# Causal decay attention into a gated feed-forward net: the order of work where the one hands over to the other, the order of two weight loads, and x in six arrays instead of one

## The chip, the cores and the metric

The kernel runs on one core of a Trainium2 chip. The metric is the device time of one execution in microseconds; the median of three executions stands for a kernel. A profiled execution gives a trace of every instruction; its span (first to last record) is a little shorter than its device time.

## The reference

Inputs are q, k and v of 8 batches x 8 heads x 576 tokens x 64, a forget factor f per token, and two weights. Cut to what matters:

```python
scores = q @ k.T / 8
cum = cumsum(log(clip(f, 1e-4, 1)))
scores = where(causal, -1e9, scores + cum[:, None] - cum[None, :])
attn = softmax(scores)
x = (attn @ v), heads side by side             # 4608 tokens x 512
h = x @ w_in                                   # 512 x 2048
g = h * erf(softplus(h))
y = g @ w_out                                  # 2048 x 512
```

## The kernel before

**Attention.** A pair is two heads of one batch; there are 32 pairs, p = 0 to 31, and each is done in two halves, t = 2p and 2p + 1, so t runs from 0 to 63 (`NH` is 64). Half t goes through stages in successive turns of one loop: scores on TensorE and their reduction on VectorE (turn t), exponentials on ScalarE (t + 1), `normalize` on GpSimd (t + 2), `transposes` on TensorE into PSUM banks of a ring of three and `evacuate` out of them (t + 3), `values` on TensorE (t + 4), and `store`, VectorE copies out of PSUM (t + 4 or t + 5). The transposes of an even half fill three banks (12 matmuls), those of an odd half four (13). `values` has one PSUM bank, so the next `values` waits for the copies of `store`. The odd half's store issues one DMA that writes 128 rows x 576 tokens of x to the DRAM array `xt_d` (512 x 4608). `evacuate` uses ScalarE for banks 0 and 1 and VectorE for 2 and 3. Turns 64 to 67 (the loop runs to `NH + 4`) drain the last halves.

**Feed-forward.** Tokens are taken 768 at a time (a visit k), features 256 at a time; one such piece is a unit u, 48 in all. A unit is `up(u, 0)` and `up(u, 1)` (42 matmuls into four PSUM banks a, b, x, y; seven products of a Strassen-like scheme with each operand split into a high and a low part), `activate` (ScalarE: four softplus, four erf, with a table load ahead of each kind), `gate` (VectorE: erf times h), `round_gate` (ScalarE rounds to the high part `gh`, GpSimd subtracts for the low part `gl`), and `down` (36 matmuls with `wo`, the weights of w_out, into `y`). One PSUM bank per name a, b, x, y exists, so `up(u + 1)` waits for the last reader of the bank of unit u; that of bank a is gate 0. `load_wi` and `load_wo` fetch a unit's weights from DRAM into two SBUF buffers each. `load_x` fetches a visit's x in four quarters from `xt_d`; `sub`, `high` and `low` make operands of it on GpSimd and ScalarE.

**The handover.** Turns 64 and 65 put `up(0, 0)` and `up(0, 1)` among the last attention halves; turn 65 ends with `activate(0)` and the gates of unit 0; turn 66 transposes half 63, does `values(62)`, then `up(1, 0)`; turn 67 does `up(1, 1)`, then `values(63)` and its store. After the loop come the pools of the feed-forward stage (`wop` is the first of them, where attention's pool `wk` lay, whose first tiles are the probabilities `pr`), `load_wo(0)`, `load_wo(1)`, `load_wi(3)`, and then, for each unit, `middle` (down, activate and gates of the next unit), and `up(u + 2)`.

**What sets the order.** TensorE, VectorE, ScalarE and GpSimd run in the order in which the Python code issues their instructions. SP, which issues all DMAs but one, is not in that list (`ORDERED`): the framework's planner puts its DMAs in order by when it thinks they can start, and SP then takes them strictly one after another, waiting for each. Each DMA uses one of eight semaphores in turn, so it also waits for the DMA eight before it.

Of the kernel before, what the change touches and what calls it, by code (L numbers as in the profile page):

```python
# [11 lines left out]
F32 = mybir.dt.float32  # L12
# [9 lines left out]
P = 128  # L22
B, H, S, D = 8, 8, 576, 64
NT = B * S
DM = H * D
# [27 lines left out]
TB = 384  # L53
NW = 2 * TB
NV = NT // NW
# [18 lines left out]
class Moe:  # L74
# [38 lines left out]
    def load_x(self, k):  # L113
        if k >= len(self.visits):
            return
        for nm in ("11", "12", "22", "21"):
            i, j = int(nm[0]) - 1, int(nm[1]) - 1
            self.raw[k, nm] = r = self.half(nm, k)
            c = self.visits[k][0] * NW + j * TB
            self.nc.sync.dma_start(out=r, in_=self.xt_d[2 * i * P:2 * (i + 1) * P, c:c + TB]  # L120
                                   .rearrange("(k p) t -> p k t", p=P))

    def sub(self, k, name, kds=range(2)):
# [34 lines left out]
    def load_wo(self, u):  # L158
        if u < self.n:
            self.wo[u] = w = self.wop.tile([P, 2, 2, DM], F32R, name=f"wo{u}", tag="wo", bufs=2)  # L160
            self.nc.sync.dma_start(out=w.rearrange("p f h e -> p (f h e)").bitcast(F32),
                                   in_=self.wo_d[self.units[u][2]])

    def up(self, u, part):
        nc = self.nc
# [145 lines left out]
def attention_moe(ctx, tc, q2, k2, vp, f, w_in, w_out, out):  # L311
    nc = tc.nc
# [6 lines left out]
    dram = ctx.enter_context(tc.tile_pool(name="dram", bufs=1, space=DRAM))  # L319
# [11 lines left out]
    tiny = edge.tile([P, EDGE], F32, name="edge")  # L331
    nc.vector.memset(tiny, 1e-9)
    cum_d = dram.tile([B * H, S], F32, name="cum_d")
    xt_d = dram.tile([DM, NT], F32, name="xt_d")

    part_d = [dram.tile([P, DM], F32, name=f"part_d{c}") for c in range(NTB * HALF)]
    wi_d = [dram.tile([P, 2 * 7 * 2 * P], F32, name=f"wi_d{a}") for a in range(NU)]
# [6 lines left out]
    moe = Moe(tc, xt_d, out, xp, wp)  # L344
# [106 lines left out]
    with ExitStack() as ph:  # L451
# [18 lines left out]
        def load(p):  # L470

            q = io.tile([P, PAD + S], F32, name=f"q{p}", tag="q")
            k = io.tile([P, S], F32, name=f"k{p}", tag="k")
            nc.sync.dma_start(out=q, in_=q2[p // NP, p % NP])
            nc.sync.dma_start(out=k, in_=k2[p // NP, p % NP])
            c = io.tile([P, 2, S], F32, name=f"c{p}", tag="c")
            if p:
                for j in range(2):
                    n = 2 * p + j
                    nc.sync.dma_start(out=c[:, j], in_=cum_d[n:n + 1].rearrange("a s -> (a s)").partition_broadcast(P))  # L480
            pairs[p] = [q, k, c]
# [65 lines left out]
        def transposes(t, a):  # L547

            half = t % 2
            if a == 0:  # L550
                pts[t] = wk.tile([P, 1600 if half else 1536], F32, name=f"pt{t}", tag=f"pt{half}", bufs=1)
            banks[t, a] = b = ps_t.tile([P, 512], F32, name=f"t{t}_{a}", tag="t")
            for n, (i, j, *ch) in enumerate(BANKS[half][a]):

                at = TOFF[i] + (i * P if j is None else 2 * END[i] - ch[0] * P - P if j else ch[0] * P)
                nc.tensor.transpose(out=b[:, n * P:(n + 1) * P], in_=probs[t][:, at:at + P], identity=ident)  # L556

        def evacuate(t, a):
            b, pt = banks.pop((t, a)), pts[t]
            if a == 3:  # L560
                nc.vector.tensor_copy(out=pt[:, 1536:], in_=b[:, 64:128])
            elif a == 2:
                nc.vector.tensor_copy(out=pt[:, 1024:1536], in_=b)  # L563
            else:
                nc.scalar.copy(out=pt[:, 512 * a:512 * a + 512], in_=b)  # L565
            if a == len(BANKS[t % 2]) - 1:
                del probs[t]

        def values(t):


            half = t % 2
            held[t] = o = ps_o.tile([P, 512], F32, name=f"o{t}", tag="o")
            v, pt = vals[t // 2], pts.pop(t)
            parts = [(OCOL[i], P, ch, [PLACE[half][i, j, ch] for j in range(2)])
                     for i in BLOCKS[half] for ch in range(i)]
            for i in BLOCKS[half]:
                skip = 64 if i else 0
                parts.append((OCOL[i] + skip, 64, 4 + i, [PLACE[half][i, None] + skip] * 2))
            for n, (to, width, ch, at) in enumerate(parts):  # L580
                for j in range(2):
                    h = slice(64 * j, 64 * j + 64)
                    nc.tensor.matmul(out=o[h, to:to + width], lhsT=v[:, ch, h], rhs=pt[:, at[j]:at[j] + width],  # L583
                                     start=n == 0, stop=n == len(parts) - 1, skip_group_check=True)

        def store(t):
            p, half = divmod(t, 2)
            o = held.pop(t)
            if half == 0:
                held["x"] = xo = wk.tile([P, S], F32, name=f"xo{p}", tag="xo")  # L590
                blocks = xo[:, 64:].rearrange("p (a q) -> p a q", a=4)
                nc.vector.tensor_copy(out=blocks[:, ::3], in_=o[:, :256].rearrange("p (a q) -> p a q", a=2))
            else:
                xo = held.pop("x")
                nc.vector.tensor_copy(out=xo[:, 192:448], in_=o[:, :256])
                nc.vector.tensor_copy(out=xo[:, :64], in_=o[:, 256:320])
                b, pp = divmod(p, NP)
                queue = nc.sync if t < NH - 1 else nc.scalar
                queue.dma_start(out=xt_d[pp * P:(pp + 1) * P, b * S:(b + 1) * S], in_=xo)
                del vals[p]  # L600

        NH = B * H
# [20 lines left out]
        def units(t):  # L623
            moe.up((t - NH) // 2, (t - NH) % 2)
            if t == NH + 1:
                moe.load_wi(2)

        for t in range(NH + 4):
            there = [0 <= t - n < NH for n in range(6)]
            p, half = divmod(t, 2)  # L630
            if half == 0 and t + 4 < NH:
                load(p + 2)
            if half == 0 and there[2]:
                load_values(p - 1)
            if t == X0:
                moe.load_x(0)
                moe.later = moe.x_steps(0)
            if t == NH - 6:
                moe.load_wi(0)
                moe.load_wi(1)  # L640
            if there[2]:
                normalize(t - 2)
            if there[5] and t < NH + 2:
                store(t - 5)
            if t in (NH, NH + 1, NH + 3):
                units(t)
            if there[0]:
                scores(t)
            if there[1]:
                exps(t - 1, 0)  # L650
            if there[0]:
                reduce(t, 0)
            if there[3]:
                for a in range(3):
                    transposes(t - 3, a)
                evacuate(t - 3, 0)
            if there[3] and len(BANKS[(t - 3) % 2]) == 4:
                transposes(t - 3, 3)
            if there[4]:
                values(t - 4)  # L660
            if there[1]:
                exps(t - 1, 1)
            if there[0]:
                reduce(t, 1)
            if there[3]:
                for a in range(1, len(BANKS[(t - 3) % 2])):
                    evacuate(t - 3, a)
            due = 2 * t + 2 if t < 4 else 8 + (8 * NU1 - 4) * (t - 3) // (NH - 4)
            while work and 8 * NU1 + 5 - len(work) < due:
                convert(work.pop(0))  # L670
            if t > X0 and moe.later:
                convert([moe.later.pop(0)])
            if t > NH and there[4]:
                store(t - 4)
            if t == NH + 1:
                moe.activate(0)
                for n in range(4):
                    moe.gate(0, n)
                    moe.round_gate(0, n)
            if t == NH - 1:  # L680
                moe.load_x(1)
            if t == NH + 2:
                units(t)
                moe.sub(1, "T1")
                moe.sub(1, "T2")
            if t == NH + 3:
                moe.sub(1, "12")
                moe.high(1, 0)
                moe.low(1, 0)
            if t == NH - 1:  # L690
                early.close()
                moe.ep = moe_pools.enter_context(tc.tile_pool(name="ep", bufs=2, side="right", reuse_waits="tile"))
                moe.ps_h = moe_pools.enter_context(tc.tile_pool(name="ps_h", bufs=1, space=PSUM, side="right", reuse_waits="tile"))
        assert not work and not moe.later and not pts and not held and not vals

    moe.wop = ctx.enter_context(tc.tile_pool(name="wop", bufs=1, reuse_waits="tile"))
# [1 line left out]
    moe.yp = ctx.enter_context(tc.tile_pool(name="yp", bufs=1, reuse_waits="tile"))  # L698
    moe.ps_y = ctx.enter_context(tc.tile_pool(name="ps_y", bufs=1, space=PSUM, reuse_waits="tile"))
    moe.load_wo(0)  # L700
    moe.load_wo(1)
    moe.load_wi(3)
    moe.want_y(0)
    work = beside_units()
    for u in range(moe.n):
# [42 lines left out]
```

## Time and profile before

| | |
|---|---|
| median of 3 runs | 1126.76 us (1122.62 to 1127.01) |
| profiled execution | 1127.5 us, of which its span is 1125.7 us |
| TensorE busy | 1086.0 us, 96% |
| VectorE, ScalarE, GpSimd busy | 835.3, 711.1, 633.5 us |
| mean granted TensorE clock | 0.98 of full |

In the profile PE is TensorE's matmuls and PEld its weight loads, DVE is VectorE, ACT ScalarE, POOL GpSimd, SP the engine that issues DMAs (SPq is its queue). A row of the timeline has a start and a duration in us, the engine, the line, the operation, what it writes and reads (`out<-in`, buffer numbers left out), its shape and how many instructions were merged; in brackets stands the idle time of the engine before it and what ended that. `s` are scores, `pr` probabilities, `t` and `pt` their transposes in PSUM and SBUF, `o` values, `xo` the piece of x to be stored, `pha`, `phb`, `phx`, `phy` the four banks of up, `u` sums of them, `e` the gated activations, `y` the result of down. Rows of the chain of waits have start, duration, and what the end of the program hung on.

### The profile page before, as it was taken

The page shows a single profiled execution, that of the slowest core. Times are in us where ns is not written, and L with a number is a line of the kernel's source. Part 1 is how long each engine was busy: PE and PEld are TensorE (multiplying, and loading weights), DVE is VectorE, ACT ScalarE, POOL GpSimd, SP SyncE. Part 2 cuts the span into 40 slices and gives each one's busy share as a digit, 9 for nine tenths or more (in the row PEclk, how much of TensorE's full clock was granted, in tenths as well). Part 3 has the DMA queues.
Part 4 walks back from the last instruction along what each step waited for, and adds up shares of the span by engine and source line. Part 5 has one row for each costly group of instructions (what it writes and reads, how often), then busy time and mean ns, then how long its engine had stood idle before and what let it go on. Part 6 is the DMA issues. An engine that isn't in the chain of part 4 may idle for free.

```text
span 1125.7 us, 21838 instructions
## 1 busy us (share of the span) xinstructions
PE 1086.0 (96%) x7552; PEld 957.9 (85%) x7552; DVE 835.3 (74%) x1940; ACT 711.1 (63%) x1540; POOL 633.5 (56%) x758
## 2 busy tenths in 40 slices
PE   5999989999999699999999999999999999999998
PEld 3788878788888598899998899888999889999897
DVE  7798868989996289999766877866556765566665
ACT  3687867788887456666666646665555665545553
POOL 1665656878875567787873755553443433433322
PEclk7899989999999799999999999999999999999999
DMA  8698898888875567969786786876655745465532
GB/s 294 202 331 281 287 386 281 300 269 265 288 279 189 194 209 287 346 225 360 257 325 211 288 311 255 320 252 221 222 178 195 260 171 204 169 234 206 178 132 93
DMA packets 75725, 280.11 MB, mean 249 GB/s; under 512 B 7904, under 2 KB 17120, under 8 KB 63328
## 3 DMA queue, kind: packets, MB, share of 16 engines
q1 hardware_dynamic: 75472, 278.43, 70.0%
q8 instruction: 60, 0.98, 0.3%
q14 instruction: 49, 0.40, 0.1%
q10 hardware_dynamic: 144, 0.29, 0.1%
HBM read 231.88 MB, written 46.81 MB: 248 GB/s over the span
## 4 chain that ended last, share of the span: by engine, by line
PE 89%; DVE 4%; DMA 4%; ACT 1%; issue 1%; POOL 0%; SPq 0%; POOLq 0%; DVEq 0%; ACTq 0%
PE y L233 35%; PE pha L175 9%; PE phx L175 9%; PE phy L175 9%; PE s L498 8%; PE o L583 7%; PE t L556 6%; PE phb L175 4%; DMA v<-in_vp_dram 3%; PE s L503 2%; DVE pr L521 1%; DMA wo<-wo_d 1%; DVE pt L563 0%; DMA fd<-in_f_dram 0%; DVE wtop L366 0%
## 5 line engine op out<-in xcount | busy, mean ns | idle before, releaser
L222 POOL TENSOR_TENSOR gl<-e,gh 128x384 fp32r<-128x384 f32 x192 | 218.5, 1169 | 354.0 <-PE y L233 245.2
L233 PE MATMUL y<-wo,gh 128*128 128x512 f32 x1152 | 357.4, 391 | 8.9 <-DMA wo<-wo_d 8.9
L233 PEld LDWEIGHTS y<-wo,gh 128*128 128x128 f32 x1152 | 215.9, 188 | 53.3 <-DMA wo<-wo_d 9.1
L544 POOL TENSOR_SCALAR pr<-pr,st 128x576 f32<-128x576 f32 (+4 forms) x320 | 164.1, 534 | 120.7 <-DVE st L540 67.5
L233 PE MATMUL y<-wo,gl 128*128 128x512 f32 x576 | 225.5, 392 | 0.0
L254 DVE TENSOR_TENSOR ys<-y,ys 128x512 f32<-128x512 f32 x252 | 172.6, 688 | 69.1 <-PE y L233 69.1
L533 ACT ACTIVATE pr<-pr,st 128x576 f32<-128x576 f32 (+3 forms) x320 | 176.7, 556 | 3.7 <-DVE st L521 3.7
L521 DVE CUSTOM_DVE_ANT_0 pr<-s,c 128x576 f32<-128x576 f32 (+3 forms) x320 | 136.3, 486 | 28.7 <-PE s L503 17.4
L498 PE MATMUL s<-k,q 64*128 64x320 f32 (+4 forms) x768 | 122.0, 432 | 15.1 <-DMA k<-in_k_dram 7.7
L221 ACT CAST gh<-e 128x384 fp32r<-128x384 f32 x192 | 93.9, 513 | 67.2 <-DVE e L214 65.3
L233 PEld LDWEIGHTS y<-wo,gl 128*128 128x128 f32 x576 | 108.4, 188 | 22.9
L204 ACT ACTIVATE e<-pha 128x384 f32<-128x384 f32 x48 | 23.6, 491 | 155.3 <-PE pha L175 155.3
L498 PEld LDWEIGHTS s<-k,q 64*128 64x128 f32 x768 | 81.0, 198 | 46.4 <-issue 22.2
L204 ACT ACTIVATE e<-u 128x384 f32<-128x384 f32 x144 | 74.8, 522 | 70.1 <-DVE u L181 68.0
L565 ACT COPY pt<-t 128x512 f32<-128x512 f32 x128 | 73.6, 576 | 71.3 <-PE t L556 67.5
L175 PE MATMUL pha<-xs,wi 128*128 128x384 f32 x576 | 117.5, 339 | 0.0
L175 PE MATMUL phx<-xs,wi 128*128 128x384 f32 x576 | 115.3, 334 | 0.0
L175 PE MATMUL phy<-xs,wi 128*128 128x384 f32 x576 | 115.3, 334 | 0.0
L583 PE MATMUL o<-pt,v 128*64 128x128 f32 (+1 forms) x1920 | 105.1, 263 | 6.8 <-DMA v<-in_vp_dram 4.3
L583 PEld LDWEIGHTS o<-pt,v 128*64 128x64 f32 x1920 | 96.3, 139 | 16.8 <-DVE st L521 5.6
L556 PE MATMUL t<-ident,pr 128*128 128x128 f32 x800 | 105.6, 279 | 5.1 <-DVE pt L563 4.8
L175 PEld LDWEIGHTS pha<-xs,wi 128*128 128x128 f32 x576 | 103.0, 189 | 3.8
(68 smaller groups left out, 1658.7 us busy)
## 6 DMA issues: line engine op xcount, KB each, us to landing
wi<-wi_d SPq DMA_DIRECT2D x48, 1792.0 KB, 7.8
wo<-wo_d SPq DMA_DIRECT2D x48, 1024.0 KB, 5.1
v<-in_vp_dram SPq DMA_DIRECT2D x32, 576.0 KB, 7.4
c<-cum_d SPq DMA_DIRECT2D x62, 288.0 KB, 6.1
r<-xt_d SPq DMA_DIRECT2D x36, 384.0 KB, 4.9
q<-in_q_dram SPq DMA_DIRECT2D x32, 320.0 KB, 5.7
k<-in_k_dram SPq DMA_DIRECT2D x32, 288.0 KB, 6.0
out_dram<-ys SPq DMA_DIRECT2D x36, 256.0 KB, 4.7
```

The costliest lines, as they stand in the source:

```text
L175: nc.tensor.matmul(out=ps, lhsT=wi[:, w, n, kd], rhs=xs[:, x, kd], start=not part and kd == 0 and i == 0, stop=kd == 1 and i == 2, skip_gr ...
L204: nc.scalar.activation(out=e_, in_=h[c], func=AF.Softplus)
L221: nc.scalar.copy(out=gh, in_=e_)
L222: nc.gpsimd.tensor_tensor(out=gl, in0=e_, in1=gh.bitcast(F32), op=ALU.subtract)
L233: nc.tensor.matmul(out=y, lhsT=x[:, cs], rhs=wo[:, i, w], start=i == 0 and n == 0, stop=i == 1 and n == 2)
L254: nc.vector.tensor_tensor(out=ys, in0=y, in1=ys, op=ALU.add)
L498: nc.tensor.matmul(out=s[j][:, at:at + k1 - k0], lhsT=q[h, PAD + START[i]:PAD + END[i]], rhs=k[h, k0:k1], start=i > 0, stop=k1 < END[i])
L521: nc.vector.tensor_tensor_reduce(out=to[:, ::-1] if j else to, in0=score, in1=decay_, scale=-0.125, scalar=BIG, op0=ALU.add, op1=ALU.min, ...
L533: nc.scalar.activation(out=seg, in_=seg, func=AF.Exp, bias=st[:, 0, j, m:m + 1], scale=-1.0, accum_out=st[:, 1, j, m:m + 1])
L544: nc.gpsimd.tensor_scalar(out=seg, in0=seg, scalar1=st[:, 2, j, m:m + 1], scalar2=1.0, op0=ALU.mult, op1=ALU.mult)
L556: nc.tensor.transpose(out=b[:, n * P:(n + 1) * P], in_=probs[t][:, at:at + P], identity=ident)
L583: nc.tensor.matmul(out=o[h, to:to + width], lhsT=v[:, ch, h], rhs=pt[:, at[j]:at[j] + width], start=n == 0, stop=n == len(parts) - 1, skip ...
```

## The change

Three things are changed.

- After turn 65 the loop ends. Written out behind it: `activate(0)`; the transposes of half 63 with their evacuation, now all four on VectorE (`t == NH - 1`); `values(62)`; the fourth transpose; `store(62)`; the last evacuation; `values(63)`; the gates of unit 0; `store(63)`; the subtractions and the first operand of visit 1; and only then `up(1, 0)` and `up(1, 1)`.
- `load_wi(3)` is tied behind `load_wo(1)` on SP's queue.
- x lies in six DRAM arrays of 512 x 768. The store of a pair whose batch reaches over a multiple of 768 tokens (batches 1, 2, 5 and 6, 16 pairs) becomes two DMAs, of 192 and 384 tokens or the other way round.

```diff
-            c = self.visits[k][0] * NW + j * TB
-            self.nc.sync.dma_start(out=r, in_=self.xt_d[2 * i * P:2 * (i + 1) * P, c:c + TB]
+            x = self.xt_d[self.visits[k][0]]
+            self.nc.sync.dma_start(out=r, in_=x[2 * i * P:2 * (i + 1) * P, j * TB:(j + 1) * TB]
...
-    xt_d = dram.tile([DM, NT], F32, name="xt_d")
+    xt_d = [dram.tile([DM, NW], F32, name=f"xt_d{v}") for v in range(NV)]
...
-            elif a == 2:
-                nc.vector.tensor_copy(out=pt[:, 1024:1536], in_=b)
+            elif a == 2 or t == NH - 1:
+                nc.vector.tensor_copy(out=pt[:, 512 * a:512 * a + 512], in_=b)
             else:
                 nc.scalar.copy(out=pt[:, 512 * a:512 * a + 512], in_=b)
...
                 queue = nc.sync if t < NH - 1 else nc.scalar
-                queue.dma_start(out=xt_d[pp * P:(pp + 1) * P, b * S:(b + 1) * S], in_=xo)
+                for v in range(b * S // NW, (b * S + S - 1) // NW + 1):
+                    c0, c1 = max(b * S, v * NW), min(b * S + S, v * NW + NW)
+                    queue.dma_start(out=xt_d[v][pp * P:(pp + 1) * P, c0 - v * NW:c1 - v * NW],
+                                    in_=xo[:, c0 - b * S:c1 - b * S])
...
-        for t in range(NH + 4):
+        for t in range(NH + 2):
...
-            if t in (NH, NH + 1, NH + 3):
+            if t >= NH:
                 units(t)
...
-            if t == NH + 1:
-                moe.activate(0)
-                for n in range(4):
-                    moe.gate(0, n)
-                    moe.round_gate(0, n)
             if t == NH - 1:
                 moe.load_x(1)
-            if t == NH + 2:
-                units(t)
-                moe.sub(1, "T1")
-                moe.sub(1, "T2")
-            if t == NH + 3:
-                moe.sub(1, "12")
-                moe.high(1, 0)
-                moe.low(1, 0)
...
+        last = NH - 1
+        moe.activate(0)
+        for a in range(3):
+            transposes(last, a)
+            evacuate(last, a)
+        values(last - 1)
+        transposes(last, 3)
+        store(last - 1)
+        evacuate(last, 3)
+        values(last)
+        for n in range(4):
+            moe.gate(0, n)
+            moe.round_gate(0, n)
+        store(last)
+        for name in ("T1", "T2", "12"):
+            moe.sub(1, name)
+        moe.high(1, 0)
+        moe.low(1, 0)
+        for part in range(2):
+            moe.up(1, part)
...
     moe.load_wo(0)
-    moe.load_wo(1)
-    moe.load_wi(3)
+    with tc.issue_after(moe.load_wo(1).ins):
+        moe.load_wi(3)
```

`load_wo` now returns its DMA, which the last lines need.

More of the change, by code (lines that the diff above doesn't have):

```diff
@@ L160, in load_wo @@
             self.wo[u] = w = self.wop.tile([P, 2, 2, DM], F32R, name=f"wo{u}", tag="wo", bufs=2)
-            self.nc.sync.dma_start(out=w.rearrange("p f h e -> p (f h e)").bitcast(F32),
-                                   in_=self.wo_d[self.units[u][2]])
+            return self.nc.sync.dma_start(out=w.rearrange("p f h e -> p (f h e)").bitcast(F32),
+                                          in_=self.wo_d[self.units[u][2]])
     def up(self, u, part):
```

## The prediction

> **What bounds the kernel now.** I read the page first, for the busiest engine.
>
> ```profile
> span 1125.7 us, 21838 instructions
> PE 1086.0 (96%) x7552; PEld 957.9 (85%) x7552; DVE 835.3 (74%) x1940; ACT 711.1 (63%) x1540; POOL 633.5 (56%) x758
> ```
>
> TensorE is the bound, so only its idle time and its slow spells can be won. Next, what TensorE waited for, longest first (total, times, longest):
>
> ```profile
> PE y L233 <- DMA wo<-wo_d: 8.9, 1, 8.9
> ...
> PE o L583 <- DMA v<-in_vp_dram: 4.3, 3, 2.9
> ```
>
> The first is a single wait; the second will matter for attention. The timeline of TensorE at the handover shows where the first lies, and another:
>
> ```profile
> 352.22 1.72 PE L556 MATMUL t<-ident,pr 128*128 128x128 f32 x13
> 353.87 1.54 PE L583 MATMUL o<-pt,v 128*64 128x128 f32 x28
> 355.34 1.31 PE L175 MATMUL pha<-xs,wi 128*128 128x384 f32 x6
> ...
> 359.98 1.66 PE L583 MATMUL o<-pt,v 128*64 128x128 f32 x32
> 361.57 1.53 PE L556 MATMUL t<-ident,pr 128*128 128x128 f32 x12
> 367.93 0.45 PE L556 MATMUL t<-ident,pr 128*128 128x128 f32 x1 [4.84 <-DVE pt L563]
> 368.31 2.83 PE L583 MATMUL o<-pt,v 128*64 128x128 f32 x28
> ...
> 379.25 1.66 PE L583 MATMUL o<-pt,v 128*64 128x128 f32 x32
> 389.86 1.22 PE L233 MATMUL y<-wo,gh 128*128 128x512 f32 x2 [8.95 <-DMA wo<-wo_d]
> ...
> 399.69 1.23 PE L175 MATMUL pha<-xs,wi 128*128 128x384 f32 x6
> ...
> 406.99 0.63 PE L233 MATMUL y<-wo,gh 128*128 128x512 f32 x2
> ```
>
> At 361.57 the last half (63) starts its transposes; the fourth waits 4.84 us, and the 28 value matmuls behind the wait take 2.83 us where they took 1.54 at 353.87: TensorE also runs slow after a long idle. At 380.9 everything is done for `down(0)` but the weights, which come 8.95 us later. `up(2)` starts at 399.69. Behind that nothing is left to win, as the chain in order of time shows: from here down starts every 15.5 us.
>
> ```profile
> 407.15 8.20 PE y L233 x36
> 422.66 8.20 PE y L233 x36
> ```
>
> So the question is when `up(2)` starts: 38.12 us after 361.57 now.
>
> **The change part by part.**
>
> *The floor.* Between 361.57 and the start of `up(2)` stand the same matmuls in either order. At full speed, taken as start to next start in the rows above: transposes of an odd half 353.87 - 352.22 = 1.65, even values 355.34 - 353.87 = 1.47, odd values 361.57 - 359.98 = 1.59, an up 406.99 - 399.69 = 7.30, a down 15.51 - 7.30 = 8.21. Sum 20.2 us, against 38.1: at most 17.9 us can go.
>
> *The transposes' wait.* It was for VectorE's copy of a bank, and that copy stood behind the gates of unit 0, which waited for ScalarE:
>
> ```profile
> 362.02 0.21 DVE L596 COPY xo<-o 128x64 f32<-128x64 f32 x1
> 365.23 0.56 DVE L214 TENSOR_TENSOR e<-e,pha 128x384 f32<-128x384 f32 x1 [2.99 <-ACT e L206]
> ...
> 367.11 0.68 DVE L563 COPY pt<-t 128x512 f32<-128x512 f32 x1
> ```
>
> Now three copies follow 362.2 at once: 0.6 to 0.7 each, done by 364.2, in time VectorE spent idle. TensorE: transposes to 363.1, values(62) to 364.6 (its bank was emptied at 362.23), the fourth transpose to 364.8. Then values(63) needs that one bank again: store(62) is one copy of 256 columns, which I call 0.4 (an estimate between the 0.21 of 64 columns and the 0.68 of 512 above), and the last evacuation one of 64 columns, 0.21. I take 0.8 us of idle with the handovers; 0.4 if the copy alone counts, 1.0 if all is in series. values(63) ends at about 367.2.
>
> *What could be late next: the gates.* They move behind these copies, to about 365.4 to 367.4, against 365.23 on. `up(1, 0)` needs bank a, free after gate 0 at 366.0: before 367.2, so no wait. The gates' readers are ScalarE's casts, then GpSimd:
>
> ```profile
> 366.45 1.28 ACT L207 ACT_TABLE_LOAD   x1
> 367.75 1.75 ACT L221 CAST gh<-e 128x384 fp32r<-128x384 f32 x4
> 368.34 3.89 POOL L222 TENSOR_TENSOR gl<-e,gh 128x384 fp32r<-128x384 f32 x4 [7.92 <-ACT gh L221]
> ```
>
> The casts wait for the table load until 367.75 in either order, so `gl` is done by 372.2 as before. `up(1)` takes 367.2 to 374.5. `down(0)` finds its operands 2.3 us early. ScalarE loses two copies and keeps its place. The three subtractions and the first operand of visit 1 (eight instructions) stay behind `gl` on GpSimd; at the 0.97 us of the four above that is to 380. With three more ahead of it `gl` of unit 1 comes at some 383 to 387, before `down(1)` at 382.7 + 7.3 = 390 (below).
>
> *The weights.* SP's rows around it, and the landing times (KB each, median us from issue to landing):
>
> ```profile
> 360.86 0.38 SPq L155 DMA_DIRECT2D wi<-wi_d  x1
> 362.27 0.32 SPq L599 DMA_DIRECT2D xt_d<-xo  x1
> 379.36 0.32 SPq L155 DMA_DIRECT2D wi<-wi_d  x1
> 379.72 0.90 SPq L161 DMA_DIRECT2D wo<-wo_d  x2
> ```
>
> ```profile
> wi<-wi_d SPq DMA_DIRECT2D x48, 1792.0 KB, 7.8
> wo<-wo_d SPq DMA_DIRECT2D x48, 1024.0 KB, 5.1
> v<-in_vp_dram SPq DMA_DIRECT2D x32, 576.0 KB, 7.4
> xt_d<-xo SPq DMA_DIRECT2D x31, 288.0 KB, 7.3
> wi_d<-wa SPq DMA_DIRECT2D x8, 512.0 KB, 3.0
> ```
>
> The load of wi at 379.36 waited for the end of `up(1)`, and both wo loads stood behind it with SP idle since 362.6. They were issued before values(63) ended, so they need no tile that values(63) or store(63) still read; what remains are the probabilities, last read by the fourth transpose at 364.8. The first wo load then goes out between 362.6 and 365. In the old place wi and wo together took 389.86 - 379.36 = 10.5 us to land. Counted from the wi load at 360.86, that gives 371.4; add 1 us for the store between them: 372.4. Counted from the latest issue, 365 + (389.86 - 379.72) = 375.1. TensorE wants it at 374.5, so it costs between nothing and 0.6 us; I take nothing, since the load in front has a start of 1.7 to 4 us here, against 0.36 there. wi for unit 3 now goes out at 374.5 behind both, 24 us before `up(3)`.
>
> *The sum.* `down(0)` runs from 374.5 at full speed (no idle above 1 us ahead of it) to 382.7. 399.69 - 382.7 = 17.0 us, which is 17.9 less the 0.8 of idle.
>
> *The split stores.* 16 more DMAs on SP, at the 0.32 us of the row above 5 us of issue in all, while SP waits most of the time. What can matter is when SP is held, because v loads queue behind. In the chain:
>
> ```profile
> 136.19 8.91 DMA v<-in_vp_dram
> 145.25 2.83 PE o L583 x28
> 148.07 3.00 PE s L498 x12
> ...
> 157.79 1.47 PE o L583 x28
> 159.26 1.66 PE s L498 x12
> ...
> 259.51 1.47 PE o L583 x28
> ```
>
> and in SP's waits and timeline:
>
> ```profile
> SPq L120 <- DMA xt_d<-xo: 17.2, 4, 7.3
> ```
>
> ```profile
> 246.56 0.38 SPq L486 DMA_DIRECT2D v<-in_vp_dram  x1
> ```
>
> A load of x held SP until a store of x had landed; the v load behind it went out late, and TensorE lost 2.93 us of waiting (the longest of the three v waits) and 1.36 + 1.34 us of slow running: 5.6 us. Undisturbed, a v load has 259.51 - 246.56 = 13.0 us and needs 7.4, so a hold costs nothing up to about 5.6 us. The split leaves the first x load waiting for a smaller store; the planner may place these loads elsewhere too. Bounds: -5.6 us (this hold gone) to +5.6 (one more like it). I take 0: a third of a store lands hardly sooner, since landing goes with the traffic and not with the size (512 KB in 3.0 us, 288 KB in 7.3).
>
> The Trainium skill, page "DMA: Bandwidth & Descriptors", section "Anatomy of one DMA", gives each DMA about 2 us of fixed cost beside its bytes (fitted on GpSimd's path): an estimate by it is 16 x 2 = 32 us more, which speaks against this part. Were all of it on TensorE's path the sum would be 15 us slower; the row of 3.0 us for 512 KB agrees with the fixed part, and no row shows it reaching TensorE.
>
> Against the profiled execution: 1127.5 - 17.0 = 1110.5 us. That one lies 0.7 above the median of the runs, so I forecast 1109.8, rounded to 1110.
>
> **The rivals.**
>
> - *A hold less in attention.* The load of x no longer delays v: 1110 - 5.6 = 1104. For it: the wait is there; against: the order of loads and stores stays.
> - *A hold more, or wo lands last.* One more hold gives 1115.5. If wo lands after the 8.9 to 10.5 us of these rows plus 2 us more from an issue at 365, TensorE idles some 2.5 us and starts down slowly (the first down took 9.83 us, 399.69 - 389.86, against 8.21), 4 us in all: 1114.
> - *The loads keep their order.* wi still goes first, after `up(1)` at 374.5, and wo lands 10.5 us later at 385.0: down(0) starts only 4.9 us earlier, 1122. Against it: nothing on SP's path to wo waits for `up(1)`.
> - *Slower: SP is held again and again in attention.* A split store takes one more of the eight semaphores, SP waits for the DMA eight before, v loads slip past their 5.6 us of cover, and each such pair costs TensorE 5.6 us. From five of the 16 pairs on the change is slower (5 x 5.6 = 28, less 17): 1138. Against it: only three v waits in 32 pairs now.
>
> **How the numbers follow.** Forecast (1108 to 1112.5): 0.50. A hold less: 0.17. A hold more or wo late: 0.24. Order kept: 0.05. Slower: 0.04. A change of 0.5% (5.6 us) is about the least that can be told from none here: faster 0.50 + 0.17 + 0.24 = 0.91, same 0.05, slower 0.04. The range takes in the first three, with 1 us on either side of the one and 1.5 of the other: 1103 to 1117.
>
> **What would show it.** The new trace should have: no wait of TensorE for wo and none above 1 us from the last half's transposes to the second up; values(62) near 1.5 us; wo issued ahead of wi within 3 us of the store of pair 30; the first down at about 8.2 us and beginning some 13 us after these transposes (15 less in the absolute), and `up(2)` 17 us earlier. I am wrong if TensorE waits there for `gl`, for bank a or for wo, or if the gain at the handover is seen and v waits of attention have grown or gone.

## The result, and the profile after

| | median us | fastest to slowest |
|---|---|---|
| before, 4 runs | 1124.69 | 1121.76 to 1127.01 |
| after, 4 runs | 1105.72 | 1103.85 to 1106.66 |

The ratio is 0.9839, with a 95% interval of 0.9818 to 0.986: 16 to 20 us faster. Forecast were 1110 us and a gain of 17.0 us; the time lies inside the stated range of 1103 to 1117, though not between the 1108 and 1112.5 to which the text gave its 0.50. The profiled execution of the changed kernel took 1103.85 us, its span is 1102.1.

The top of the page after, and from its waits of TensorE the first, the one for v, and the last:

```profile
span 1102.1 us, 21862 instructions
PE 1078.5 (98%) x7552; PEld 951.9 (86%) x7552; DVE 842.7 (76%) x1942; ACT 710.8 (64%) x1538; POOL 636.7 (58%) x758
```

```profile
PE s L498 <- DMA k<-in_k_dram: 8.0, 1, 8.0
...
PE o L583 <- DMA v<-in_vp_dram: 1.1, 2, 0.7
...
PE y L233 <- DVE ys L252: 0.2, 1, 0.2
```

The 8.9 us for wo and the 4.8 us for the transposes are gone, and the waits for v fell from 4.3 to 1.1 us. The timeline of TensorE after, over the handover:

```profile
354.86 1.53 PE L556 MATMUL t<-ident,pr 128*128 128x128 f32 x12
356.32 1.54 PE L583 MATMUL o<-pt,v 128*64 128x128 f32 x28
357.80 0.33 PE L556 MATMUL t<-ident,pr 128*128 128x128 f32 x1
358.39 1.66 PE L583 MATMUL o<-pt,v 128*64 128x128 f32 x32 [0.27 <-DVE xo L592]
359.98 1.33 PE L175 MATMUL pha<-xs,wi 128*128 128x384 f32 x6
...
367.39 0.63 PE L233 MATMUL y<-wo,gh 128*128 128x512 f32 x2
...
375.59 1.23 PE L175 MATMUL pha<-xs,wi 128*128 128x384 f32 x6
```

From the last half's transposes to `up(2)` it is 375.59 - 354.86 = 20.73 us, against 38.12. I call this stretch the handover below. All its matmuls run back to back but for 0.27 us. The windows of the two kernels over their handovers (length, then busy us of PE, PEld, DVE, ACT and POOL with their instructions, granted clock, DMA share, GB/s), after first, then before:

```profile
354.86:375.59 20.73, 20.46 (x155) 18.52 (x152) 16.15 (x29) 15.93 (x28) 13.95 (x14) 1.00 0.86 321
```

```profile
361.57:399.69 38.12, 24.34 (x156) 21.53 (x152) 14.58 (x29) 17.16 (x31) 17.15 (x18) 0.82 0.49 182
```

TensorE's busy time fell by 3.9 us for the same matmuls, because the granted clock went from 0.82 to 1.00, and its idle time by 13.5. The DMA engines, half idle before, are at 0.86.

VectorE's copies of the last half and the first gate, and SP's rows, after:

```profile
355.62 1.89 DVE L563 COPY pt<-t 128x512 f32<-128x512 f32 x3
357.91 0.42 DVE L592 COPY xo<-o 128x256 f32<-128x256 f32 x1 [0.40 <-PE o L583]
358.25 0.21 DVE L561 COPY pt<-t 128x64 f32<-128x64 f32 x1
358.53 0.55 DVE L214 TENSOR_TENSOR e<-e,pha 128x384 f32<-128x384 f32 x1
```

```profile
354.16 0.39 SPq L155 DMA_DIRECT2D wi<-wi_d  x1
355.56 0.32 SPq L601 DMA_DIRECT2D xt_d<-xo  x1
355.98 2.50 SPq L161 DMA_DIRECT2D wo<-wo_d  x2
367.58 0.32 SPq L155 DMA_DIRECT2D wi<-wi_d  x1
```

The first wo load goes out 0.1 us after the store of pair 30, the next wi after `up(1)`. The DMA view cut to that first load gives its landing time (KB, us):

```profile
wo<-wo_d SPq DMA_DIRECT2D x1, 1024.0 KB, 10.4
```

It lands at 366.4, 1.0 us before TensorE wants it at 367.39.

Between the profiled executions lie 1125.7 - 1102.1 = 23.6 us of span. The handover is 17.4 of them. Behind it the changed kernel is 0.5 slower; ahead of it lie 361.57 - 354.86 = 6.7, of which 5.5 arise at one place, between scores 24 and 26 (of 64), where the kernel before waited 2.93 us for v and ran slow. In the trace after, SP and TensorE there:

```profile
121.35 0.79 SPq L601 DMA_DIRECT2D xt_d<-xo  x2
127.23 0.89 SPq L120 DMA_DIRECT2D r<-xt_d  x2
...
132.23 0.39 SPq L486 DMA_DIRECT2D v<-in_vp_dram  x1
```

```profile
140.50 1.54 PE L583 MATMUL o<-pt,v 128*64 128x128 f32 x28 [0.38 <-DVE st L521]
```

The load of x still holds SP behind a store, for 5 us; but v was there in time. These two traces don't say whether the split stores did that.

### The profile page after: what moved, and what is told of

Same layout as the page of the kernel before. It is cut to its first block, busy times and chain, and to the rows that moved or that the text cites. A ratio compares the mean times of both kernels' runs of the same rounds, so it can differ in the third digit from the quotient of the medians.

```text
span 1102.1 us, 21862 instructions
## 1 busy us (share of the span) xinstructions
PE 1078.5 (98%) x7552; PEld 951.9 (86%) x7552; DVE 842.7 (76%) x1942; ACT 710.8 (64%) x1538; POOL 636.7 (58%) x758
## 4 chain that ended last, share of the span: by engine, by line
PE 59%; DVE 0%; ACT 0%; issue 0%; DVEq 0%; ACTq 0%
PE y L233 32%; PE pha L175 8%; PE phx L175 8%; PE phy L175 8%; PE phb L175 4%; DVE wa L382 0%; ACT L206 0%; DVE u L181 0%; ACT e L206 0%; DVE ys L254 0%; DVE ys L252 0%; ACT e L204 0%; DVEq L252 0%; DVEq L214 0%; DVEq L181 0%
## 5 line engine op out<-in xcount | busy, mean ns | idle before, releaser
L498 PE MATMUL s<-k,q 64*128 64x320 f32 (+4 forms) x768 | 119.5, 425 | 14.5 <-DMA k<-in_k_dram 8.0
L204 ACT ACTIVATE e<-pha 128x384 f32<-128x384 f32 x48 | 23.6, 491 | 153.2 <-PE pha L175 151.4
L583 PE MATMUL o<-pt,v 128*64 128x128 f32 (+1 forms) x1920 | 102.5, 259 | 4.3 <-DVE xo L592 2.0
L583 PEld LDWEIGHTS o<-pt,v 128*64 128x64 f32 x1920 | 93.8, 137 | 14.0 <-DVE st L521 6.2
```

Source lines behind the costliest of these rows:

```text
L204: nc.scalar.activation(out=e_, in_=h[c], func=AF.Softplus)
L498: nc.tensor.matmul(out=s[j][:, at:at + k1 - k0], lhsT=q[h, PAD + START[i]:PAD + END[i]], rhs=k[h, k0:k1], start=i > 0, stop=k1 < END[i])
```

## The experiments

Theory: the handover is the whole gain, and in it SP's order (wo behind a DMA that waits) and VectorE's order (evacuation behind the gates) are two separate causes. Rivals: the split stores carry part of it; the tie of wi does; the place of values(63) does by itself. Ratios are to the kernel before run beside each; their intervals are of 95%. Behind each stand the handover as the profile gives it and TensorE's wait for wo.

| kernel | median us | ratio | interval | handover us | wait for wo us |
|---|---|---|---|---|---|
| before | 1123.16 to 1124.69 | 1 | | 38.12 | 8.95 |
| after | 1105.72 | 0.9839 | 0.9818 to 0.986 | 20.73 | none |
| after, run again | 1103.96 | 0.9824 | 0.9807 to 0.9841 | 20.71 | none |
| arrays only | 1122.47 | 0.9993 | 0.998 to 1.0006 | 38.66 | 9.4 |
| handover only | 1104.60 | 0.9824 | 0.9807 to 0.9841 | 20.73 | none |
| tie only | 1111.47 | 0.9885 | 0.9868 to 0.9903 | 26.77 | none |
| before, x loads later | 1121.87 | 0.9982 | 0.9971 to 0.9993 | 38.25 | 9.3 |
| after, evacuation on ScalarE | 1112.35 | 0.9908 | 0.9891 to 0.9925 | 26.07 | none |
| after, x loads later | 1105.05 | 0.9849 | 0.9834 to 0.9864 | 20.73 | none |
| after, up first | 1121.02 | 0.999 | 0.9976 to 1.0004 | 37.17 | 13.9 |
| after, wi first | 1125.35 | 1.003 | 1.0013 to 1.0046 | 41.88 | 18.2 |
| after, up first, wo first | 1104.75 | 0.9828 | 0.9809 to 0.9847 | 21.67 | none |
| handover only, x loads later | 1103.71 | 0.982 | 0.9803 to 0.9837 | 20.71 | none |
| after, wo(1) before wo(0) | 1105.93 | 0.9839 | 0.9822 to 0.9856 | 22.49 | 1.6 |

**The arrays alone.** The kernel before with the first, second and fourth hunk of the diff: six arrays, split stores.

> Only the third part: the kernel before with x in six arrays and the 16 stores split. The trace after gained 17.4 us at the handover and 6.8 us ahead of it, 5.5 of these where SP was held by a load of x until a store of x had landed. Theory A, the split shortens that hold (the quarter waits for 96 KB, not 288 KB): no v wait above 1 us, median 3 to 6 us below the kernel before (about 1119 to 1121). Theory B, the hold comes and goes by execution and the split has no part in it: within 2 us of the kernel before, executions from 1121 to 1128 as there. The handover stays: waits of 4.8 us on the fourth transpose and 8.9 us on wo.

0.9993, and single runs from 1121.08 to 1126.62, as of the kernel before (1120.94 to 1127.86): theory B. The wait of 2.93 us for v is not in this trace at that length, nor in those of the kernels with one array that follow: here TensorE waits 1.6 us at that place, with the handover alone 1.0 at most and with the tie alone 0.5. Nor do six arrays keep it away: in one of the changed kernels below (evacuation on ScalarE) it was 2.56 us. In the profiled execution of before the last half's transposes begin at 361.57, those of all other profiled kernels between 354.2 and 357.2.

**The handover alone.** The changed kernel with these hunks undone, and without the tie:

```diff
-    with tc.issue_after(moe.load_wo(1).ins):
-        moe.load_wi(3)
+    moe.load_wo(1)
+    moe.load_wi(3)
```

> Only the first part: the new order at the handover with all four evacuations on VectorE, one array for x, and no tie between the loads of wo and wi. Handover theory: values(63) is issued before up(1), so the planner itself puts wo ahead of wi; from the last half's transposes to up(2) 20.7 us against 38.1, that is 17.4 us less, median near 1107. Theory A of the split adds that the long v wait stays (1107 to 1110); theory B that it comes and goes (1104 to 1109). Rival: without the tie wi goes first again and wo lands 10.5 us behind the end of up(1): a gain of about 5 us only, 1120.

20.73 us, the whole gain: 0.9824. SP's rows of this kernel have the order of the changed one without being told:

```profile
357.34 2.50 SPq L161 DMA_DIRECT2D wo<-wo_d  x2
368.95 0.32 SPq L155 DMA_DIRECT2D wi<-wi_d  x1
```

So beside the new order of the handover neither the arrays nor the tie bring anything that these runs can tell.

**The tie alone.** The kernel before with the last hunk only.

> Only the second part: the kernel before with wi(3) tied behind wo(1). If wo was late only because it stood behind wi on SP: both wo loads go out at 362.6 to 365, down(0) follows values(63) with no wait, and it runs in 8.2 instead of 9.8 us: 8.95 + 1.6 = 10.5 us less, median near 1114; the 4.8 us wait on the fourth transpose stays, with the slow spell behind it. If wo is held by something else in the old order (a tile that values(63) still reads), SP issues it near 381 and there is no gain: 1124.

The waits for wo go, the wait of the transposes stays. TensorE's rows:

```profile
362.10 0.45 PE L556 MATMUL t<-ident,pr 128*128 128x128 f32 x1 [4.85 <-DVE pt L563]
362.48 2.71 PE L583 MATMUL o<-pt,v 128*64 128x128 f32 x28
...
372.60 1.66 PE L583 MATMUL o<-pt,v 128*64 128x128 f32 x32
374.19 0.72 PE L233 MATMUL y<-wo,gh 128*128 128x512 f32 x2
```

The handover is 11.35 us shorter than before (10.5 expected), and the other 26.77 - 20.73 = 6.04 us are the transposes' part: 4.85 of waiting and the slow spell behind it, that is, matmuls at a lower granted clock (0.54 over the 28 of `values(62)`). Some 0.8 of the 11.35 are not the queue's: the slow spell behind the transposes' wait ended sooner in this trace, so that `values(62)` and `up(1)` took 10.1 us together against 10.9 before. In the old order, then, the queue was somewhat under two thirds of the loss and VectorE's order somewhat over one third.

**The hold by itself.** The kernel before, and further down the changed one, with the loads of visit 0's x tied behind a later DMA:

```diff
+            if p == 12:
+                held["v12"] = dma
...
-                moe.load_x(0)
+                with tc.issue_after(held.pop("v12").ins):
+                    moe.load_x(0)
```

> The hold by itself: the kernel before, with the four loads of visit 0's x tied behind the v load of pair 12, when all stores that they read have landed long ago. Hold theory: SP waits no more for a store of x (17.2 us in 4 waits before), the v wait of 2.9 us and the slow spell behind it go, and every execution is like the fastest ones of before: median 1119 to 1122. Rival, v is late because the DMA engines are busy with other loads and not because SP was held: the v wait stays, no change, 1124.

0.9982, 1.8 us by the medians (1121.87 against 1123.66), and single runs from 1119.96 to 1123.63 where the kernel before went up to 1127.86. In its trace no load of x waits for a store any more, and TensorE never waits for v. That fits a small price of holding SP in some executions; it doesn't show it, as the loads also stand at another place now.

> The changed kernel with the four loads of visit 0's x tied behind the v load of pair 12. In the kernel before the same tie gave 1.8 us (0.9982). If what it removes is the holds of SP in attention, it gives the same here: 1103 to 1104.5, a narrow spread, no wait of SP for a store of x. If the split stores had removed the holds already, nothing is left to gain: 1105 to 1106.

1105.05, between the two measurements of the changed kernel (1103.96 and 1105.72): nothing that can be told from noise. Its trace has no wait of SP for a store of x ahead of a load of x, and still one of TensorE for v, of 2.1 us at 315.78. Holding SP behind a store of x is therefore not the only way in which v comes late. This v was issued at 304.87, after SP had stood 5.5 us for a store of wtop, and took 10.8 us to land; the kernel before and the changed one have that wait of SP too (6.0 and 5.5 us), and there the same load landed in 9.1 and 9.3 us. Why the landing took longer isn't settled.

**The engine of the evacuation.**

```diff
-            elif a == 2 or t == NH - 1:
+            elif a == 2:
```

> The changed kernel with the first two evacuations of the last half back on ScalarE. They then stand behind the softplus, both table loads and the erf of unit 0, which end at 361.05 in the trace after, so values(63) cannot start before about 362.2 where it started at 358.39. Theory, the evacuations set the handover: some 3.5 to 5 us of idle ahead of values(63) or of the fourth transpose, slow matmuls behind it, 4 to 6 us lost, handover 25 to 27 us, median 1109 to 1112. Rival, up(1) would be held by bank a or by gl anyway and the engine of the evacuation is no matter: 20.7 us, 1105.

5.3 us more of handover, 26.07, and 1112.35:

```profile
362.83 3.52 PE L583 MATMUL o<-pt,v 128*64 128x128 f32 x32 [3.56 <-ACT pt L565]
```

values(63) waited 3.56 us for ScalarE's copies behind the activations and ran at half speed. The move to VectorE is needed.

**The place of values(63).** The changed kernel with `values(last)` and `store(last)` behind the two calls of `up(1, part)`.

> The changed kernel with up(1) ahead of values(63) again, as in the kernel before; evacuations on VectorE, gates behind them and the tie of wi behind wo stay. If the gain comes from the evacuation no longer standing behind the gates and from wo ahead of wi, and not from where values(63) stands: up(1) waits some 1.2 us for gate 0 and values(63) for nothing, handover 21 to 21.5 us, median 1105 to 1106.5. If the place of values(63) matters by itself, the handover is longer by 2 us or more.

Neither: the handover was 37.17 us and the time 1121.02, as if nothing had been changed. Not TensorE's own order did it, but SP's queue:

```profile
354.87 0.32 SPq L601 DMA_DIRECT2D xt_d<-xo  x1
374.32 0.32 SPq L394 DMA_DIRECT2D wo_d<-wtop  x1
374.74 0.88 SPq L161 DMA_DIRECT2D wo<-wo_d  x2
375.71 0.38 SPq L155 DMA_DIRECT2D wi<-wi_d  x1
```

```profile
381.45 1.19 PE L233 MATMUL y<-wo,gh 128*128 128x512 f32 x2 [13.86 <-DMA wo<-wo_d]
```

The tie holds, wi stands behind wo. But another DMA stands ahead of both: a store of converted weights (`wtop`) that GpSimd has ready only at 374.3. SP waited for it from 355.2 on; the next run shows that wo could have gone. The next run ties that store, too, behind wo:

```diff
-        moe.middle(u, lambda u, place: convert(work.pop((u, place), ())))
+        with tc.issue_after(wo1.ins) if u == 0 else ExitStack():
+            moe.middle(u, lambda u, place: convert(work.pop((u, place), ())))
```

> The kernel with up(1) ahead of values(63), with one thing more: the DMAs of middle(0) on SP's queue, the store of wtop among them, are tied behind wo(1) too. In the run without this SP stood from 354.9 to 374.3 for wtop, which GpSimd delivers last, with both wo loads behind it. If that place on the queue was all that was wrong: wo goes out within 4 us of the store of pair 30, no wait for wo above 1 us, handover 21 to 21.8 us (1.0 us of it a wait for gate 0), median 1105 to 1107. If values(63) ahead of up(1) matters by itself, because wo needs a tile that values(63) reads: wo still goes out after 367 and the handover stays above 30 us.

21.67 us and 1104.75. Its rows of SP and, with the wait for bank a, of TensorE:

```profile
356.16 0.32 SPq L601 DMA_DIRECT2D xt_d<-xo  x1
356.57 2.50 SPq L161 DMA_DIRECT2D wo<-wo_d  x2
```

```profile
359.74 1.31 PE L175 MATMUL pha<-xs,wi 128*128 128x384 f32 x6 [1.02 <-DVE e L214]
```

On TensorE the place of values(63) is worth 21.67 - 20.73 = 0.9 us, the wait for gate 0 that it covers. The rest comes through SP: with values(63) behind `up(1)`, in the order that the change gives the rest, the planner puts wtop ahead of wo, and with values(63) ahead of `up(1)` wo comes first without any tie. The place of values(63) doesn't decide that by itself, though: with the tie alone it also stood behind `up(1)`, and there the first wo load went out right behind the store:

```profile
356.84 6.06 SPq L161 DMA_DIRECT2D wo<-wo_d  x2
```

How the planner reckons is in no trace.

**The price of the queue.** The tie the other way round:

```diff
-    moe.load_wo(0)
-    with tc.issue_after(moe.load_wo(1).ins):
-        moe.load_wi(3)
+    with tc.issue_after(moe.load_wi(3).ins):
+        moe.load_wo(0)
+        moe.load_wo(1)
```

> The changed kernel with the tie the other way round: both wo loads behind wi(3). wi(3) waits for the end of up(1) at 367.4, wo lands 10 to 10.5 us behind it (10.5 in the trace before), so down(0) starts near 378 with a wait of 10 us and runs in 9.8 us instead of 8.2: handover 32 to 33 us, median 1117 to 1118. That is the price of the queue order alone. Rival, DMAs of one queue overlap enough that wo, the smaller, lands with wi: a wait of 7 us, 1113.

It was dearer than that: 41.88 us of handover, 1125.35, slower than the kernel before (1.003, interval 1.0013 to 1.0046). SP and TensorE:

```profile
375.91 0.32 SPq L394 DMA_DIRECT2D wo_d<-wtop  x1
376.32 0.38 SPq L155 DMA_DIRECT2D wi<-wi_d  x1
376.75 21.39 SPq L161 DMA_DIRECT2D wo<-wo_d  x3
```

```profile
386.58 1.19 PE L233 MATMUL y<-wo,gh 128*128 128x512 f32 x2 [18.16 <-DMA wo<-wo_d]
```

The store of wtop had moved ahead here too, which held wi for 8 us after `up(1)`; behind it wo took the 10 us expected (386.6 - 376.3; the row of wo also holds the load for unit 2, issued much later). Two DMAs that wait, put ahead of wo, cost more than the whole change had won.

**How thin the cover is.** Both tiles are allocated as before, and the DMA of wo(1) is issued first:

```diff
-    moe.load_wo(0)
-    with tc.issue_after(moe.load_wo(1).ins):
+    for u in range(2):
+        moe.wo[u] = moe.wop.tile([P, 2, 2, DM], F32R, name=f"wo{u}", tag="wo", bufs=2)
+    with tc.issue_after(moe.load_wo(1).ins):
+        last_wo = moe.load_wo(0)
+    with tc.issue_after(last_wo.ins):
         moe.load_wi(3)
```

> The changed kernel with the load of wo(1) issued ahead of that of wo(0), to see how thin the cover of wo(0) is. In the trace after, wo(0) went out at 355.98 and took 10.4 us: 366.4, 1.0 us before TensorE wanted it at 367.39; wo(1), which waits for the fourth transpose, went out at 358.2 and took 11.1. Now wo(0) lands where wo(1) did, near 369.5: a wait of 2 to 3 us for wo, no more, and the first down at about its 8.2 us; handover 23 to 23.8 us, median 1107 to 1108. If the cover were as thick as the 2.1 us that was predicted and the loads shared the engines evenly, the wait would be below 1 us.

```profile
371.06 0.70 PE L235 MATMUL y<-wo,gh 128*128 128x512 f32 x2 [1.55 <-DMA wo<-wo_d]
```

A wait of 1.6 us, a little under the 2 to 3 expected; handover 22.49, and 1105.93 against 1103.96 of the changed kernel beside it. SP's row:

```profile
357.93 2.50 SPq L163 DMA_DIRECT2D wo<-wo_d  x2
```

The second of the two, now wo(0), went out at 360.11, right after the fourth transpose (360.08) and 2.2 us behind the first, and landed 10.8 us later. With the 1.0 us of cover and the 1.6 of waiting it comes 2.6 us later than in the changed kernel; how much of that is the later issue and how much the 1 MB in front, this run doesn't separate. Second in the queue, wo(0) is no longer covered.

**The smallest set, and the change once more.** The handover alone with the x loads later, and the changed kernel on the same chip.

> The new handover without the tie of wi, one array for x, and the loads of visit 0's x tied behind the v load of pair 12: the smallest set of edits that carries the gain, with the 1.8 us that the tie gave in the kernel before. If the holds cost 1 to 2 us in the median in this order too: 1102.5 to 1104, below the changed kernel run beside it. If they do not: 1104.5 to 1105.5, the same as the handover alone.

> The changed kernel as it is, beside the others on one chip: 1104.5 to 1106. If the arrays and split stores are neutral in the new order as they were in the old one (0.9993), it lies within 1 us of 1104.6, the handover alone.

1103.71 and 1103.96, ratios of 0.982 and 0.9824: the same. No version here beats the changed kernel by more than these runs can tell; the first needs neither the arrays nor the tie.

## Why the prediction was right

**The floor and the handover: right.** 20.2 us were reckoned as floor and 21.1 as the new length; it is 20.73, a gain of 17.4 instead of 17.0. The idle ahead of values(63), taken as 0.8, is nearer the lower end that I gave, 0.4: from the fourth transpose at 357.80 to values(63) at 358.39 it is 0.59 us, of which a transpose needs some 0.12 to 0.2. VectorE's copy of `xo` set it, and the small evacuation went beside it in part.

**The gates, the casts and gl: right.** Put on the time axis of the kernel before (6.71 us later), gate 0 began at 365.2 (about 365.4 forecast) and bank a was free before `up(1)` wanted it. The run with up first shows what that step is worth when it is uncovered: 1.0 us. The run with the evacuation on ScalarE shows what the other step, the copies on VectorE, is worth: 3.6 us of waiting and a slow spell. One margin was thinner than forecast: `gl` of unit 1 ended at 382.43, which is 389.1 on that axis and not 383 to 387, 0.5 us before `down(1)` began. GpSimd worked without a pause from 361.64 until then, with the subtraction for wtop among its steps.

**The weights: right by 1 us.** wo was forecast to land 2.1 us before it is wanted; it was 1.0. Issue came at the early end, but landing took 10.4 us from there; counted from the wi load in front it is 366.4 - 354.16 = 12.2, where 11.5 had been put together from 10.5 and 1.

**Why wo comes first: right in the outcome, not in the reason.** The text held that the tie and the waits on tiles decide, and that nothing on SP's path to wo waits for `up(1)`. The path is the planner's order, and that is no property of the tiles: with the tie kept and values(63) moved back, SP waited 19 us for a store that I had not looked at. The rival "the loads keep their order", priced at 1122, has its like in the run with up first (1121.02); with wi first it came out slower than before, since I had counted only wi, and the store of wtop stood there as well.

**The split stores: right at nothing.** 0.9993, with an interval of 0.998 to 1.0006. Thirds and two thirds of a store landed no sooner than whole ones: the DMA view after, for whole, two-third and one-third stores:

```profile
xt_d<-xo SPq DMA_DIRECT2D x15, 288.0 KB, 7.4
...
xt_d<-xo SPq DMA_DIRECT2D x16, 192.0 KB, 7.6
xt_d<-xo SPq DMA_DIRECT2D x16, 96.0 KB, 7.3
```

The estimate of 32 us by the fixed cost of the page "DMA: Bandwidth & Descriptors" of the Trainium skill never reached TensorE.

**The size: the base was off.** The forecast was 1110 and 1105.7 came. 0.4 us of the 4.3 is the handover. Most of the rest is in the step "against the profiled execution": I took 17.0 from an execution that held the 5.6 us stall of v, and corrected by 0.7 for the median of three runs. I had weighed that stall as something the change might remove (a hold less, 0.17) and not as something that comes and goes with the execution. The kernel before has a median of 1123.66 over the 23 runs beside the first experiments, 3.1 us below the 1126.76 from which I started; with that base the same steps give 1106.7, and 1106.3 with the 17.4 of the handover. The last 0.6 us are within what two measurements of the changed kernel differ by (1105.72 and 1103.96). That it is the stall which most executions of the kernel before lack is inferred: it was profiled once, and only kernels with the same or nearly the same attention were seen without it. So the mechanism of the handover was right, and that the range of 1103 to 1117 held the time owes something to luck: the measured 1105.7 lies nearest to the rival "a hold less" (1104). The stall of v was indeed absent, but nothing here makes the change the reason: the arrays alone gave 0.9993.

## What to carry to other kernels

A queue that is served strictly in order is part of the critical path: look at every DMA that a change lets slip ahead of the one that is needed, not only at the one that stood there before, and read the order from the trace. Where an engine's copy stands behind a step that waits for a third engine, moving the copy ahead of it is worth the wait and, on TensorE here, the slow spell that followed. And before a small gain is read off one profiled execution, see whether its stalls stand in the next one too.

## What was not expected of the hardware

**A slow spell does not follow from the length of a wait alone.** Behind 2.93 us of waiting the 28 matmuls of `values` took 2.83 us (before); behind 2.56 us they took 1.54 (evacuation on ScalarE, in attention), and behind 2.12 us, 2.29, with the scores slow as well (after, x loads later). The granted clock over these matmuls was 0.50, 1.00 and 0.63 of full. The rows of the last two kernels:

```profile
142.20 1.54 PE L583 MATMUL o<-pt,v 128*64 128x128 f32 x28 [2.56 <-DMA v<-in_vp_dram]
```

```profile
315.78 2.29 PE L585 MATMUL o<-pt,v 128*64 128x128 f32 x28 [2.12 <-DMA v<-in_vp_dram]
318.00 2.60 PE L500 MATMUL s<-k,q 64*128 64x448 f32 x12
```

The Trainium skill, page "TensorE: Matmul & The Clock Gate", section "What's actually happening", has TensorE's activity watched in windows of about 3.4 us that run freely; that fits waits whose effect depends on when they fall, but no run here moves a wait alone. Its rule under "HAM oscillation — how this bites in real kernels", no idle gaps above some 3.4 us, is too wide for this kernel: here 2.1 us sufficed once.

**VectorE slowed beside GpSimd.** With the handover packed closer, three elementwise steps on the weights fell beside GpSimd's subtractions. One of them, before (GpSimd idle) and after (GpSimd at work), and GpSimd's row after:

```profile
381.89 0.43 DVE L365 TENSOR_SCALAR wtop<-wtop 128x512 f32<-128x512 f32 x1
```

```profile
368.81 1.12 DVE L365 TENSOR_SCALAR wtop<-wtop 128x512 f32<-128x512 f32 x1
```

```profile
367.47 2.18 POOL L129 TENSOR_TENSOR rT<-r,rT 128x384 f32<-128x384 f32 x2
```

0.43 us became 1.12. The same holds in the changed kernel's second run. It isn't new, either: this step runs 32 times in a program, and in the trace before 16 of the 32 fall into GpSimd's idle time and take 0.43 us each, the other 16 beside GpSimd's work, and take 0.83 to 1.40; after, it is 12 and 20, with the same times. DMAs in flight don't explain it: with seven of them and GpSimd idle it took 0.43 (at 154.73 before), with none and GpSimd at work 1.40 (at 439.23). The Trainium skill says that the two engines share their way into SBUF (page "GPSIMD Engine Reference", section "Specifications"), with contention for some kinds of VectorE instruction; the trace agrees for this one. TensorE hardly feels it: its last wait above, 0.2 us at 450.78, stands behind three such steps that took 3.6 us instead of 1.3; before, they were as slow at that place, without a wait.
